# Sixty loads issued from ScalarE's program instead of SyncE's, with a new written order

## The chip, the cores and the metric

One core of a Trainium2 chip runs the whole kernel. The metric is the device time of one execution in microseconds (us), as the median of several runs. The engines are PE (TensorE, matrix products; PEld is its weight load), DVE (VectorE), ACT (ScalarE), POOL (GpSimd) and SP (SyncE), which here does nothing but issue DMA transfers. SPq is SP's program as the trace shows it.

## What is computed

Three layers in a row, in float32 precision (products are made from two-part float16 splits):

```python
# 1. delta rule attention; B, H, S, D = 4, 8, 768, 48
for t in range(S):
    y[:, :, t] = q_t @ state
    v_old = state^T @ k_t                       # k normalised
    state += beta_t * outer(k_t, v_t - v_old)
# 2. gated layer on x = y (S x 384): sigmoid(conv5(x)) * (x @ w_val) @ w_out
# 3. gated MLP: h = gelu(x @ w_in); u, v = halves of h; v = layernorm(v) * g
#    out = x + (u * (w_sg @ v + b)) @ w_out2     # w_sg mixes over the 768 positions
```

## The kernel before, in words

The attention is worked in chunks of 64 positions, 12 chunks to a batch element, 48 in all (`NSEQ`). All eight heads go together: four on each half of the 128 partitions. `norm` and `keys` prepare the keys of pairs of chunks (24 pairs, `ND`), `gram`, `base` and `merge` invert the small triangular systems of the chunks, `seq` carries the state from chunk to chunk, and `attend` gives the outputs, which go by a DMA (`xd<-ys`) to a buffer in memory. The MLP functions (`front`, `value`, `hidden`, `gates`, `mix`, `final`) read that buffer in tiles of 256 positions. Their products fill PE between the short products of the recurrence; in the last stretch of the run they are alone.

Three inputs are loaded all along the run: `kf` (keys, 12 loads, in `norm`), `qf` and `vf` (queries and values of a pair of chunks, 24 each, in `load`), 60 loads together. `qf` and `vf` have two buffers (`sp`, bufs=2), `kf` has one.

No scheduler decides the order. The class `Program` records every operation, and the table `ORDER` lists for each engine in which order it issues its operations. `in_order` replays this table with a model of costs, sorts the operations by their modelled starts, and puts filler products (`filler`, matrices `minus`, onto a scratch bank `ps_state`) where the model has PE idle. Each engine then runs its list in order on the chip, and an instruction that waits holds up all behind it on its engine. All recorded operations have one source line in the profile (L108 before, L109 after), so rows are told apart by tile names.

Names that recur below: `sq` are squares of the keys; `wst`, `wv` are staged weights; `rh`, `wh`, `ws`, `ps_q`, `ps_state` belong to the recurrence (`ws<-wh` is a DMA that spreads a result into a block frame); `m1p`, `tbd` are frames of the triangular inverses, filled by small DMAs from `gx`, `tah`; `ys` is the output tile of a pair and `xd` its buffer in memory; `kj` are key frames; `qh`, `mh` are split queries and scores.

Of the kernel before, what the change touches and what calls it, by code (L numbers as in the profile page):

```python
# [21 lines left out]
class Op:  # L22


    def __init__(self, index, engine, method, call, kw):
        self.index, self.engine, self.method, self.call, self.kw = index, engine, method, call, kw
        self.before, self.after, self.stage, self.due = set(), [], None, 0
        self.ready = self.end = 0.0
        self.blocks = engine == "tensor" and kw["lhsT"].shape[0] <= 64 == kw["lhsT"].shape[1]
        self.cost, self.time, self.port = cost(self)  # L30
# [9 lines left out]
class Program:  # L40
# [69 lines left out]
    def in_order(self):  # L110
# [14 lines left out]
        done, moved = [], 0.0  # L125
# [3 lines left out]
        def finish(op):  # L129
            for o in op.after:  # L130
                if o.engine != op.engine:
                    t = op.end + LATENCY[op.engine]
                elif op.engine == "tensor":
                    t = op.start
                else:
                    t = op.end + (LATENCY[op.engine] if op.engine == "sync" else 0.025)
                o.ready = max(o.ready, t)
                o.left -= 1

        while any(plan.values()):  # L140
            t, i = min((max(free[e], plan[e][0].ready), i) for i, e in enumerate(ENGINES) if plan[e] and not plan[e][0].left)
            e = ENGINES[i]
# [21 lines left out]
            if e in ("vector", "scalar"):  # L164
                if e in last and drains(last[e], op):
                    t = max(t, last[e].start + last[e].time)
                last[e] = op
            op.start, used, time = t, op.cost, op.time
            done.append(op)
            if e == "sync":  # L170
                used = max(used, moved - DMA_AHEAD - t)
# [41 lines left out]
class Pool:  # L213
# [5 lines left out]
    def tile(self, shape, dtype, name, tag=None, **kw):  # L219
# [326 lines left out]
def kernel(  # L546
# [32 lines left out]
    EP = C + E  # L579
# [816 lines left out]
```

## Time and profile before

| | |
|---|---|
| median of 3 runs | 647.62 us (646.28 to 649.8) |
| the profiled execution's own time | 646.62 us |
| its span in the profile | 644.7 us |
| PE busy | 575.0 us, 89% of the span |
| DVE busy | 503.1 us, 78% |
| ACT busy | 398.2 us, 62% |
| POOL busy | 179.6 us, 28% |
| DMA queue q1 (all issued by SP) | 87.72 MB, 63.0% of 16 engines' span |

Busy shares are means over stages that differ. PE does its first product at 20 us, and from there its share rises until it is nearly always busy. Issuing a DMA isn't counted as busy time, so SP has no line in the page; its issues are read from the timeline.

### The profile page before, as it was taken

What the parts mean: (1) busy time and instruction counts of PE and PEld (TensorE: products, weight loads), DVE (VectorE), ACT (ScalarE), POOL (GpSimd) and SP (SyncE); (2) the same over time, 40 slices, a digit from 0 to 9 for tenths busy, and PEclk for the clock granted to TensorE, in tenths of its full rate; (3) what the DMA queues carried; (4) which work ended last, traced back from release to release, by engine and by line L of the source; (5) the groups of instructions that cost most, each with busy time, mean ns of one, the idle gap of its engine ahead of it and who ended that gap; (6) DMA issues with size and microseconds to landing.
All of it is one profiled execution on the core that took longest, in us unless ns stands there. A gap on an engine that the chain in (4) does not pass through costs nothing. (4 is left out here: it accounts for less than half of the span.)

```text
span 644.7 us, 23559 instructions
## 1 busy us (share of the span) xinstructions
PE 575.0 (89%) x9821; PEld 473.8 (73%) x9821; DVE 503.1 (78%) x1341; ACT 398.2 (62%) x932; POOL 179.6 (28%) x204
## 2 busy tenths in 40 slices
PE   0678879779979989799999999889999999999997
PEld 0555446668767767688888689778978897877886
DVE  7898998979889998988999879899887854562222
ACT  7886697756876767775466785344948544524221
POOL 7404041126423625366001650001605010303000
PEclk9999998989999998999999999999999999999999
DMA  7664367877579776687678778788687763211121
GB/s 223 160 202 132 126 189 235 186 156 165 107 182 175 134 122 146 128 195 132 163 143 179 145 123 170 121 140 152 120 155 141 107 142 102 63 50 34 58 82 50
DMA packets 288826, 89.22 MB, mean 138 GB/s; under 512 B 250704, under 2 KB 276944, under 8 KB 288720
## 3 DMA queue, kind: packets, MB, share of 16 engines
q1 hardware_dynamic: 288720, 87.72, 63.0%
q8 instruction: 77, 1.26, 0.9%
q14 instruction: 29, 0.24, 0.1%
HBM read 51.81 MB, written 23.33 MB: 117 GB/s over the span
## 5 line engine op out<-in xcount | busy, mean ns | idle before, releaser
L108 PE MATMUL ps_mlp<-wg,vnh 128*128 128x256 f16 x864 | 112.4, 272 | 1.4 <-DVE ps_mlp L108 1.4
L108 PEld LDWEIGHTS <-vnh 128*128 128x128 f16 x864 | 80.5, 97 | 12.0 <-issue 2.1
L108 PEld LDWEIGHTS <-kj 112*128 112x128 f16 (+1 forms) x1632 | 69.2, 97 | 21.4 <-issue 12.7
L108 PEld LDWEIGHTS <-kc 64*64 64x64 f16 x1920 | 42.1, 113 | 47.5 <-DVE kc L108 20.8
L108 PE MATMUL ps_mlp<-gvh,wi 128*128 128x256 f16 x432 | 58.0, 272 | 1.2 <-ACT v L108 0.8
L108 PE MATMUL ps_mlp<-gth,w 128*128 128x256 f16 x432 | 58.8, 272 | 0.0
L108 DVE TENSOR_TENSOR tmp<-X 128x84 f32<-128x84 f32 (+12 forms) x156 | 56.1, 360 | 1.4
L108 DVE TENSOR_TENSOR X<-X,tmp 128x84 f32<-128x84 f32 (+12 forms) x156 | 54.5, 349 | 1.5
L108 PE MATMUL ps_mlp<-wi,gvh 128*128 128x512 f16 x216 | 54.7, 379 | 0.6 <-ACT gvh L108 0.4
L108 DVE SCALAR_TENSOR_TENSOR ps_mlp<-ps_mlp,gl,bs 128x256 f32<-128x256 f32 x48 | 23.4, 488 | 34.3 <-PE ps_mlp L108 33.9
L108 DVE SCALAR_TENSOR_TENSOR a<-x,cw,a 128x256 f32<-128x256 f32 x108 | 48.8, 486 | 1.6 <-ACT a L108 1.3
L108 PE MATMUL ps_mlp<-xh,wv 128*128 128x256 f16 x324 | 45.7, 272 | 2.2 <-ACT xh L108 2.1
L108 PE MATMUL ps_mlp<-gvh,wo 128*128 128x256 f16 x324 | 47.1, 272 | 0.1
L108 PEld LDWEIGHTS <-m1p 128*128 128x128 f16 x1152 | 39.5, 96 | 9.9 <-issue 5.7
L108 PE MATMUL pk<-i,kc 64*64 64x64 f16 x704 | 22.5, 200 | 27.2 <-DVE kc L108 20.0
L108 PEld LDWEIGHTS <-wi 128*128 128x128 f16 x432 | 40.3, 97 | 6.4 <-issue 1.3
L108 PEld LDWEIGHTS <-w 128*128 128x128 f16 x432 | 40.8, 98 | 5.0
L108 PE MATMUL ps_y<-qh,kj 112*128 112x64 f16 x576 | 32.8, 193 | 4.2 <-ACT ys L108 4.1
L108 POOL TENSOR_TENSOR X<-X,bm 128x1024 f32<-128x1024 f32 x5 | 11.8, 2353 | 87.4 <-DVE X L108 72.0
L108 PEld LDWEIGHTS <-ws 128*128 128x128 f16 (+1 forms) x828 | 32.2, 98 | 4.9 <-issue 3.2
L108 PEld LDWEIGHTS <-wo 128*128 128x128 f16 x342 | 31.8, 97 | 5.5 <-issue 0.9
L108 POOL TENSOR_TENSOR vnh<-v,vnh 128x512 f16<-128x512 f32 x24 | 27.9, 1170 | 25.6 <-ACT vnh L108 25.5
(165 smaller groups left out, 1451.5 us busy)
## 6 DMA issues: line engine op xcount, KB each, us to landing
keys_d<-kc SPq DMA_DIRECT2D x22, 512.0 KB, 4.1
kj<-keys_d SPq DMA_DIRECT2D x44, 256.0 KB, 5.0
wg<-wgd SPq DMA_DIRECT2D x12, 768.0 KB, 4.8
ws<-wh SPq DMA_DIRECT2D x66, 96.0 KB, 3.6
qf<-in_qt SPq DMA_DIRECT2D x24, 224.0 KB, 3.5
kf<-in_kn SPq DMA_DIRECT2D x12, 384.0 KB, 4.7
vf<-in_vn SPq DMA_DIRECT2D x24, 192.0 KB, 3.4
xd<-ys SPq DMA_DIRECT2D x48, 96.0 KB, 3.0
```

The costliest lines, as they stand in the source:

```text
L108: op.call()
```

## The change

The 60 loads of `kf`, `qf` and `vf` are issued by ScalarE (`nc.scalar.dma_start`) and no longer by SyncE. The model in `in_order` and `cost` learns that an operation can be a DMA on another engine than SP: it has the cost of a DMA, moves the same shared transfer clock, and isn't held back by transfers that are outstanding, as SP's are. `ORDER` has new tables for all engines. The frames (`tbd`, `m1p`, `ws`) are filled by GpSimd before and after. Per engine the counts are the same, but for the 60 loads (SP 60 fewer, ACT 60 more) and the fillers on PE: 268 before, 310 after, of which 140 and 128 are 128 rows high and the others 64.

```diff
+        self.dma = method == "dma_start"
...
-                    t = op.end + LATENCY[op.engine]
+                    t = op.end + LATENCY["sync" if op.dma else op.engine]
...
-            if e in ("vector", "scalar"):
+            if e in ("vector", "scalar") and not op.dma:
...
-            if e == "sync":
-                used = max(used, moved - DMA_AHEAD - t)
+            if op.dma:
+                used = max(used, moved - DMA_AHEAD - t) if e == "sync" else used
...
 ORDER = dict(
     tensor=(
-        "17:12 0 29:2 1 31 2 32 3:14 113 65:2 129:13 67 142 68 114 143 115 69 144 116:3 70 119 71 120 72 121 73 122 "
+        "0 17:14 1 31 2 32 3:14 65:5 129:6 113 135:2 114 137:7 115 144 116:4 70:2 120:2 72:2 122:4 74:3 126:2 49:3 "
...
-    out, engine = op.kw["out"], op.engine
+    out, engine = op.kw["out"], "sync" if op.dma else op.engine
...
-                nc.sync.dma_start(out=kf[:, 2 * i:2 * i + 4], in_=kn_f[:, k * n + 2 * i:k * n + 2 * i + 4])
+                nc.scalar.dma_start(out=kf[:, 2 * i:2 * i + 4], in_=kn_f[:, k * n + 2 * i:k * n + 2 * i + 4])
...
-        nc.sync.dma_start(out=qf[0:EP], in_=qt_f[:, n:n + 2])
+        nc.scalar.dma_start(out=qf[0:EP], in_=qt_f[:, n:n + 2])
...
-        nc.sync.dma_start(out=vf, in_=vn_f[:, n:n + 2])
+        nc.scalar.dma_start(out=vf, in_=vn_f[:, n:n + 2])
```

First place: the start of ACT's program. Before:

```order
1 L108 ACT_TABLE_LOAD
2 L108 ACTIVATE wh_109<-zero 128x512
3 L108 ACTIVATE sq<-kf 128x384
4 L108 ACTIVATE kj_91<-zero 128x1024
5 L108 ACTIVATE sq<-kf 128x384 x2
```

After:

```order
1 L109 DMA kf<-in_kn 128x768
2 L109 DMA vf<-in_vn 128x384
3 L109 DMA qf<-in_qt 112x512
4 L109 DMA kf<-in_kn 128x768
5 L109 DMA vf<-in_vn 128x384
6 L109 DMA qf<-in_qt 112x512
7 L109 ACT_TABLE_LOAD
8 L109 ACTIVATE wh_109<-zero 128x512
9 L109 ACTIVATE sq<-kf 128x384 x2
10 L109 ACTIVATE kj_91<-zero 128x1024
```

Six loads now stand ahead of the table load, and the second `sq` has moved ahead of the clearing of `kj`.

Second place: SP's program where the outputs of a pair in the third batch element are stored (`xd_81<-ys`, two DMAs to a pair). Before:

```order
326 L108 DMA vf<-in_vn 128x384
327 L108 DMA tbd_95<-tah 32x16x32
328 L108 DMA ws_97<-wh_109 64x16x48
329 L108 DMA xd_81<-ys 48x4x128
330 L108 DMA ws_97<-wh_109 64x16x48
331 L108 DMA qf<-in_qt 112x512
332 L108 DMA bs<-in_b_sg 128x256
333 L108 DMA tbd_94<-tah 32x16x32
334 L108 DMA xd_81<-ys 48x4x128
```

After:

```order
270 L109 DMA ws_97<-wh_109 64x16x48
271 L109 DMA tbd_95<-tah 32x16x32
272 L109 DMA xd_81<-ys 48x4x128 x2
273 L109 DMA ws_97<-wh_109 64x16x48
274 L109 DMA wg<-wgd 128x3072
275 L109 DMA bs<-in_b_sg 128x256
```

The two loads are gone from the row, and the two stores follow each other directly, where four issues stood between them.

Third place: ACT's program in the middle of the recurrence, around the two results `wh<-ps_q` and `wh<-ps_state` of a chunk. Before:

```order
642 L108 ACTIVATE mh<-ps_y 128x256
643 L108 ACTIVATE rh<-ps_q 128x192
644 L108 ACTIVATE bs<-bs 128x256
645 L108 ACTIVATE tbd_95<-ps_b 32x8x32
646 L108 ACTIVATE wh_109<-ps_q 128x4x48
647 L108 ACTIVATE wh_109<-ps_state 112x4x48
```

After:

```order
691 L109 ACTIVATE mh<-ps_y 128x256
692 L109 ACTIVATE rh<-ps_q 128x192
693 L109 DMA vf<-in_vn 128x384
694 L109 DMA qf<-in_qt 112x512
695 L109 ACTIVATE wh_109<-ps_q 128x4x48
696 L109 ACTIVATE tbd_95<-ps_b 32x8x32
697 L109 ACTIVATE bs<-bs 128x256
698 L109 ACTIVATE wh_109<-ps_state 112x4x48
```

Two loads stand between `rh` and the `wh` that follows from it, where two other activations stood before.

## Rows read from the trace of the kernel before

**Rows 1.** Page, part 1: busy time of each engine, share, instructions.

```profile
PE 575.0 (89%) x9821; PEld 473.8 (73%) x9821; DVE 503.1 (78%) x1341; ACT 398.2 (62%) x932; POOL 179.6 (28%) x204
```

**Rows 2.** Windows: stretch, PE, PEld, DVE, ACT, POOL busy (instructions), clock, DMA share, GB/s.

```profile
20.00:280.00 260.00, 223.15 (x4563) 172.11 (x4564) 230.28 (x635) 190.03 (x461) 91.11 (x95) 0.98 0.70 160
280.00:520.00 240.00, 232.19 (x4065) 200.12 (x4063) 208.41 (x553) 151.13 (x354) 62.68 (x61) 1.00 0.78 148
520.00:645.00 125.00, 119.67 (x1203) 101.59 (x1199) 48.78 (x109) 41.89 (x85) 12.98 (x14) 0.99 0.23 66
```

**Rows 3.** Waits of PE from 20 to 280 us: total us, times, longest.

```profile
PE pk L108 <- ACT kc L108: 4.3, 8, 0.8
...
PE ps_y L108 <- ACT ys L108: 2.7, 5, 0.9
PE ps_mlp L108 <- DMA wsf<-in_w_sgT: 2.2, 2, 1.6
...
PE ps_b L108 <- DMA m1p<-gx: 1.1, 1, 1.1
```

**Rows 4.** Waits of PE from 280 us to the end.

```profile
PE ps_b L108 <- DMA m1p<-gx: 2.7, 2, 1.4
PE ps_y L108 <- DMA ws<-wh: 1.9, 3, 1.4
PE ps_y L108 <- ACT ys L108: 1.4, 2, 0.7
...
PE ps_q L108 <- DMA kj<-keys_d: 0.5, 1, 0.5
```

**Rows 5.** Waits of DVE from 20 to 280 us.

```profile
DVE wh L108 <- ACT wh L108: 4.5, 7, 1.5
DVE wst L108 <- ACT wst L108: 3.8, 4, 1.5
```

**Rows 6.** SP's issues of the three loads: min/median/max ns, first and last start.

```profile
L108 SPq DMA_DIRECT2D kf<-in_kn x12: 333/423/3324, 0.8 to 263.5; - x12
...
L108 SPq DMA_DIRECT2D qf<-in_qt x24: 328/446/1677, 5.0 to 523.3; - x24
...
L108 SPq DMA_DIRECT2D vf<-in_vn x24: 358/560/2043, 3.6 to 498.9; - x24
```

**Rows 7.** SP's timeline at the second place: start us, us, issue.

```profile
464.14 0.59 SPq L108 DMA_DIRECT2D vf<-in_vn  x1
...
468.88 0.60 SPq L108 DMA_DIRECT2D qf<-in_qt  x1
...
470.85 0.62 SPq L108 DMA_DIRECT2D xd<-ys  x1
```

**Rows 8.** ACT's and PE's timeline there, [idle before <-releaser].

```profile
474.81 0.38 ACT L108 ACTIVATE ys<-ps_y 112x256 f32<-112x256 f32 x1 [2.54 <-DMA xd<-ys]
...
475.24 0.51 PE L108 MATMUL ps_y<-qh,kj 112*128 112x64 f16 x12 [0.74 <-ACT ys L108]
```

**Rows 9.** Waits of SP's own queue, whole span.

```profile
SPq L108 <- ACT qh L108: 9.8, 6, 3.9
...
SPq L108 <- DVE qh L108: 6.3, 1, 6.3
```

**Rows 10.** Timelines of the start: ACT, SP, DVE, PE.

```profile
0.80 1.28 ACT L108 ACT_TABLE_LOAD   x1 [0.80 <-PEq L1383]
...
3.98 0.52 ACT L108 ACTIVATE sq<-kf 128x384 f32<-128x384 f32 x1 [0.77 <-DMA kf<-in_kn]
...
1.71 0.43 SPq L108 DMA_DIRECT2D beta_sb<-in_beta  x1
2.19 0.43 SPq L108 DMA_DIRECT2D gl<-in_g_ln  x1
...
16.61 0.56 DVE L108 SCALAR_TENSOR_TENSOR wst<-wst 128x384 int32<-128x384 int32 x1 [1.73 <-ACT wst L108]
...
20.04 0.53 PE L108 MATMUL pk<-i,kc 64*64 64x64 f16 x12 [20.04 <-DVE kc L108]
```

**Rows 11.** Fillers on PE: line, operation, count, busy us, mean ns, idle before.

```profile
L108 PE MATMUL ps_state<-minus 128*128 128x256 f16 (+1 forms) x268 | 30.9, 278 | 0.5 <-DVE wh L108 0.5
```

More of the change, by code (lines that the diff above doesn't have):

```diff
@@ L135, in finish @@
                 else:
-                    t = op.end + (LATENCY[op.engine] if op.engine == "sync" else 0.025)
+                    t = op.end + (LATENCY["sync"] if op.dma else 0.025)
                 o.ready = max(o.ready, t)
```

391 rows, old and new, of tables (gpsimd, scalar, sync, tensor) are left out of this document.

## The prediction

> **What bounds the kernel now.** I read the page's busy shares first: PE is busy for 575.0 of 644.7 us, and no other engine above 78% [rows 1]. The table by windows then splits the span into three stages [rows 2]. From 20 to 280 us PE is busy for 223.15 of 260 us and DVE for 230.28; ACT has 190.03, that is 73%, and neither PE nor DVE is alone the limit: both wait for links of the recurrence. From 280 to 520 us PE has 232.19 of 240 us, and after 520 us 119.67 of 125 us. So from 280 us on the time is PE's own work, of which this change takes nothing away; what can move is the first 20 us, the 36.9 us in which PE stands between 20 and 280 us, and the 7.8 us until 520 us.
>
> The waits of PE say what these are made of. Early, the largest that ACT causes are 4.3 us for `kc` and 2.7 us for `ys`, and those for transfers are 2.2 us (`wsf`) and 1.1 us (`m1p`) [rows 3]. Late, transfers are most of it: `m1p` 2.7, `ws` 1.9, `kj` 0.5, and 1.4 us for `ys` [rows 4]. That `ys` is really a transfer: at one of its places ACT stands for 2.54 us until the store `xd<-ys` has landed, and PE then stands 0.74 us for ACT [rows 8]. DVE's early waits for ACT are led by 4.5 us (`wh`) and 3.8 us (`wst`) [rows 5].
>
> **The change part by part.** The planner's edited lines run before the program exists and cost the chip nothing. Bytes and shapes of the transfers stay.
>
> *SP loses 60 issues.* At the medians of their rows, 12 `kf` at 0.423, 24 `qf` at 0.446 and 24 `vf` at 0.560 us are 5.1 + 10.7 + 13.4 = 29.2 us off SP's program [rows 6]. SP isn't the limit by itself; it is worth what PE waits behind SP's transfers: 2.2 + 1.1 early, 2.7 + 1.9 + 0.5 + 1.4 late, 9.8 us together [rows 3, 4]. That is the upper bound of the gain; the lower is nothing, since a shorter queue doesn't make a transfer later. In between, the place that I followed: in the 6.7 us ahead of the store at 470.85 us SP issued a `vf` and a `qf`, 0.59 and 0.60 us each [rows 7]; without them the store goes out 1.2 us earlier, more than PE's 0.74 us there [rows 8], and in the new order the two stores have nothing between them. But only every eighth issue is a load, so not each wait has one ahead of it. I take -4.0 us, two fifths of the bound.
>
> [...]
>
> *ACT gains 60 issues.* No row shows an issue on ACT. The nearest are SP's: 0.33 us at the least, 0.42 to 0.56 at the median, 3.32 at the most [rows 6]. I take 0.43 us, as the first lone issues of the run took [rows 10]. Six stand at the start (below); the other 54 are spread evenly over the chunks, up to 523 us [rows 6], so about 54 x 260/503 = 28 fall between 20 and 280 us (12 us more on ACT) and 26 behind it. Early, PE's 4.3 + 2.7 and DVE's 4.5 + 3.8 us of waits stand against 190 us of ACT's work, 0.08 us for each us of work [rows 2, 3, 5]: 1.0 us. Some stand inside the recurrence, as the two between `rh` and `wh` at the third place, so I take +1.5 us. The bounds: if the loads only fill ACT's idle quarter, 0; if each lies on the path wherever ACT is busy, 12 x 0.73 = +9. Behind 280 us PE's own queue of MLP products hides them: PE is busy for 97% there [rows 2]; without that cover it would be 26 x 0.43 = 11 us.
>
> A wait moves with each load: its buffer must be free. On SP such waits are in the queue's list, 9.8 us for ACT's own `qh` and 6.3 us for DVE's [rows 9]. The first kind is free on ACT, whose program has passed it. The second kind would now hold what is behind the load: at the third place `wh`, for which PE and DVE wait. I cost it at nothing, since loads have some 20 activations between them and can stand late; if it bites, it is the second rival.
>
> *The start.* `kf` goes out at the same moment as before, but six issues of 0.43 us, 0.48 apart [rows 10], put the table load 2.9 us later, its end at 5.0, and with the 0.5 us of `wh` the first `sq` at 5.5 us instead of 3.98 [rows 10]: +1.5 us. The second `sq` then follows at once, and ACT's 0.77 us wait for `kf` is gone. The start ends with a chain: DVE stands 1.73 us until ACT has made `wst` (16.61 us), after which the keys are scaled and PE begins at 20.04 us [rows 10]. ACT's lateness reaches that chain unless it is regained by ACT's pauses. I take +1.0 us, bounds 0 and +1.5.
>
> *The new order and the fillers.* There are 42 more fillers; one keeps PE for 30.9 / 268 = 0.115 us [rows 11]. They stand in gaps, cost nothing there, and at most 4.8 us where a gap isn't one. What the other moved rows do I can't sum up; the products are the same. With 24 pairs of chunks and a quarter of a us won or lost at each, 6 us either way. I take 0.
>
> The sum: -4.0 + 1.5 + 1.0 + 0 = -1.5 us on the profiled execution's 646.62 us, 645.1. That execution was 1.0 us below the median of the runs, 647.62; on the median it is 646.1 us, which I predict.
>
> **The rivals.** *The relief counts in full and the order regains more* (faster). All 9.8 us of waits behind SP's transfers go, and ACT's issues vanish in its pauses, which the early stage has (27% of the time). The start takes 1.0 back and a shorter chain gives a little: about 638 us. For it: SP issues without pause at the places of the late waits. Against it: the early stage, with most of PE's idle time, hardly waits for transfers.
>
> *ACT is held up* (slower). One mechanism: an issue on ACT takes as long as SP's in a crowded stretch or longer, and activations of the recurrence wait behind it. Place: 20 to 280 us. Price: 28 issues of 0.65 us are 18 us, of which half comes through to PE over `rh`, `wh` and `kc`, +9, with the start +1.5 and a relief of only 2: about 656 us. It decides from a mean issue on ACT of about 0.6 us, or a few of 2 to 3 us as SP's longest [rows 6]. For it: DMA engines are 70 to 78% busy there [rows 2], and DVE's waits for ACT lead its list. Against it: ACT has idle time, and the loads aren't urgent. [...]
>
> *SP isn't relieved* (the change doesn't do what it says). SP's long issues come from the crowd of transfers, which stays; then the remaining issues stretch, the gain is 0, and 1.5 + 1.0 are left: about 650 us. For it: 0.33 us alone and 0.6 in a crowd [rows 6, 7].
>
> **How the numbers follow.** A measurement of this kernel can tell about 0.5%, 3.2 us, from no change: faster is below 644.4, slower above 650.9. The forecast as summed has 0.44, with its own range 641 to 651.5: 0.12 of it faster, 0.29 the same, 0.03 slower. The fast rival has 0.25, the held-up ACT 0.20, the unrelieved SP 0.11 (0.06 the same, 0.05 slower). Faster 0.37, same 0.35, slower 0.28. The range goes from 635, a little beyond the fast rival, to 657, which takes in the slow one.
>
> **What would show it.** Right: issues on ACT of about 0.4 us; PE's late waits for `m1p`, `ws` and `ys` down from 6.0 us to about 3; PE's first product at about 21 us; PE busy for 223 us or a little more between 20 and 280 us. Wrong: issues on ACT above 0.6 us, with ACT's waits replaced by longer gaps ahead of `wh` and `rh` and PE's waits for ACT doubled (second rival); SP's issues longer than before, and late waits unchanged (third); or PE's idle time between 20 and 280 us changed by over 5 us with neither, which would be the order's doing and is what my sum knows least of.

## The result and the profile after

The changed kernel takes 649.43 us (median of 20 runs, 644.93 to 657.06), the kernel before 645.67 us in its 20 runs beside it. The ratio is 1.0051 with a 95% interval of 1.003 to 1.0071: 3.3 us slower (here and below, a ratio is turned into us on 645.67). Ratios leave out the runs over 1.5% above the fastest of their kernel, so they can differ from the ratio of the medians. The forecast was 646.1 us, 1.5 us faster than the 647.62 us that it was worked out on. The profiled execution took 649.55 us, with a span of 647.7, 3.0 above that of the kernel before.

Part 1 of the page answers to [rows 1]:

```profile
PE 579.0 (89%) x9863; PEld 476.2 (74%) x9863; DVE 498.5 (77%) x1341; ACT 398.1 (61%) x932; POOL 179.5 (28%) x204
```

The windows, columns as in [rows 2]:

```profile
20.00:280.00 260.00, 219.67 (x4512) 168.76 (x4513) 223.76 (x620) 188.13 (x458) 89.23 (x97) 0.96 0.69 159
280.00:520.00 240.00, 235.94 (x4098) 203.04 (x4098) 211.76 (x569) 153.93 (x360) 66.21 (x63) 1.00 0.82 147
520.00:648.00 128.00, 122.97 (x1254) 104.32 (x1252) 51.85 (x114) 44.11 (x90) 13.16 (x14) 1.00 0.24 69
```

Between 280 and 520 us PE's idle time fell from 7.81 to 4.06 us, 3.75 less: near the 4.0 that the forecast gave to the relief of SP. But the first stage lost 3.5 us of PE time, and the end has 3.3 us more work left in it. The waits of PE from 280 us on answer to [rows 4]; `m1p` and `kj` are gone, and `m1p`, `ws` and `ys` fell from 6.0 to 2.3 us:

```profile
PE ps_y L109 <- ACT ys L109: 1.4, 2, 0.8
PE ps_y L109 <- DMA ws<-wh: 0.9, 1, 0.9
```

The start answers to [rows 10]. ACT's timeline (start us, us):

```profile
0.80 0.40 ACTq L109 DMA_DIRECT2D kf<-in_kn  x1
1.23 0.45 ACTq L109 DMA_DIRECT2D vf<-in_vn  x1
1.70 0.45 ACTq L109 DMA_DIRECT2D qf<-in_qt  x1
2.19 0.45 ACTq L109 DMA_DIRECT2D kf<-in_kn  x1
4.62 0.33 ACTq L109 DMA_DIRECT2D vf<-in_vn  x1
6.67 0.34 ACTq L109 DMA_DIRECT2D qf<-in_qt  x1
7.04 1.28 ACT L109 ACT_TABLE_LOAD   x1 [7.04 <-DMA vf<-in_vn]
8.34 0.63 ACT L109 ACTIVATE wh<-zero 128x512 f32<-128x512 f32 x1
8.87 0.51 ACT L109 ACTIVATE sq<-kf 128x384 f32<-128x384 f32 x1
```

and PE's first product:

```profile
22.82 1.06 PE L109 MATMUL pk<-i,kc 64*64 64x64 f16 x32 [16.34 <-DVE kc L109]
```

Four loads go out 0.43 to 0.49 us apart, as forecast. Then ACT stands until 4.62 and again until 6.67 us. The table load comes 6.2 us later than before, the first `sq` 4.9 and PE's first product 2.8. What ACT stands for is a semaphore. In the trace the 485 transfers that SP and ACT issue share eight semaphores for their landings, used in turn: the first eight transfers have one each, and the ninth to the thirteenth wait for those of the first to the fifth. The first `kf` landed at 4.60 and the first `vf` at 6.65 us, each 0.02 us before ACT's next load began. The built order of ACT shows the waits:

```
4 L109 DMA kf<-in_kn 128x768
5 L109 DMA vf<-in_vn 128x384 [waits DMAHW0_49]
6 L109 DMA qf<-in_qt 112x512 [waits DMAHW2_49]
7 L109 ACT_TABLE_LOAD
```

SP's `wsf` and `bs` are held in the same way, for 2.1 us to 4.78 (`beta_sb` landed at 4.77) and for 1.8 us to 6.94 (`wst`, at 6.93). Before, such holds at the start came to 0.3 us, ahead of `bs`: SP, at 0.39 to 0.46 us for each of its first twelve issues, began the ninth to the twelfth 0.14 to 0.60 us after the landings that free their semaphores, and ACT issued none.

In the run an issue on ACT took 0.34 to 0.35 us at the median of each kind (min/median/max ns), where [rows 6] had 0.42 to 0.56 on SP:

```profile
L109 ACTq DMA_DIRECT2D qf<-in_qt x24: 318/335/452, 1.7 to 507.8; - x24
...
L109 ACTq DMA_DIRECT2D vf<-in_vn x24: 334/350/457, 1.2 to 503.0; - x24
...
L109 ACTq DMA_DIRECT2D kf<-in_kn x12: 334/353/613, 0.8 to 271.2; - x12
```

SP's other 425 issues took 317.6 us together, before 315.1 (median 0.63 and 0.62 us): hardly any of the 40.7 us that the loads had taken on SP passed on to them.

### The profile page after: what moved, and what is told of

Its sections match the earlier page's. It is cut to its first block, busy times and chain, and to the rows that moved or that the text cites. A ratio compares the mean times of both kernels' runs of the same rounds, so it can differ in the third digit from the quotient of the medians.

```text
span 647.7 us, 23605 instructions
## 1 busy us (share of the span) xinstructions
PE 579.0 (89%) x9863; PEld 476.2 (74%) x9863; DVE 498.5 (77%) x1341; ACT 398.1 (61%) x932; POOL 179.5 (28%) x204
## 4 chain that ended last, share of the span: by engine, by line
PE 62%; DVE 14%; ACT 9%; DMA 7%; issue 4%; SPq 2%; POOL 1%; ACTq 1%; DVEq 0%; POOLq 0%
PE ps_mlp L109 42%; PE ps_y L109 6%; PE pk L109 4%; PE ps_q L109 4%; DVE X L109 3%; PE ps_state L109 3%; PE ps_b L109 3%; DMA xd<-ys 2%; DVE tmp L109 2%; SPq L109 2%; ACT kc L109 1%; DVE wst L109 1%; DMA vf<-in_vn 1%; DMA tbd<-tah 1%; DMA ws<-wh 1%
## 5 line engine op out<-in xcount | busy, mean ns | idle before, releaser
L109 PE MATMUL ps_mlp<-wg,vnh 128*128 128x256 f16 x864 | 111.0, 272 | 0.6 <-DVE ps_mlp L109 0.6
L109 PE MATMUL ps_mlp<-gvh,wi 128*128 128x256 f16 x432 | 55.3, 272 | 1.2 <-ACT v L109 0.8
L109 PE MATMUL ps_state<-minus 64*64 64x256 f16 (+1 forms) x310 | 34.4, 294 | 7.0 <-POOL minus L109 6.1
L109 POOL TENSOR_TENSOR rd<-va,root 128x2 f32<-128x2 f32 x12 | 8.8, 734 | 96.9 <-DVE va L109 96.9
```

Of the source, the lines that this page charges most:

```text
L109: op.call()
```

## The experiments

Each is timed beside runs of the kernel before on its own chip; given are the median, the ratio to the kernel before and its 95% interval. By the intervals a difference between two of these kernels is known to 2 to 4 us. A single profile places a cost only roughly: b_late below has the program of before, unchanged until 281 us, and yet was 4.2 us ahead of it at 271 us. Where loads move in the lists, the planner sets the fillers anew: 290 in e_move and b_move for 268 before, 320 in e_lift and 334 in e_quiet for 310 in e_start.

**The start.** Two edits of the changed kernel. e_start has the first six loads on SP, in SP's old order (`nc.scalar if n > 2 else nc.sync`, keys `if k`), the other 54 on ACT. e_four only moves ACT's fifth and sixth load behind the first two `sq`, the clearing of `kj` and the first `rh` in ACT's list.

> The changed kernel with its first six loads on SP, in the old order of SP's first twelve issues; the other 54 stay on ACT. Theory S: the table load at 0.80 us and PE at about 20 us, 2.8 us faster than the changed kernel, and with the late waits for transfers that the move removed as fast as before or up to 3 us faster. Theory O and theory A: the table load as early, but the time only 0 to 1 us better than the changed kernel.

Measured: 646.87 us, 1.0015 [0.9986, 1.0045]. ACT's timeline begins as before, and PE's first product comes at 19.69 us:

```profile
0.80 1.28 ACT L109 ACT_TABLE_LOAD   x1 [0.80 <-PEq L1374]
...
3.96 0.94 ACT L109 ACTIVATE sq<-kf 128x384 f32<-128x384 f32 x2 [0.75 <-DMA kf<-in_kn]
...
19.69 1.06 PE L109 MATMUL pk<-i,kc 64*64 64x64 f16 x32 [13.22 <-DVE kc L109]
```

> The changed kernel with one edit in ACT's order: of its first six loads the fifth and sixth (vf and qf of the second pair) stand behind the first two sq, the clearing of kj and the first rh. Theory S (the start): these two wait until a completion semaphore that an earlier transfer uses is free again, and hold the table load until 7.04 us. Without them ahead of it the table load starts at about 2.7 us and PE at about 20.5 us instead of 22.82; 2.3 to 2.8 us faster than the changed kernel, about 1 us above the kernel before. Theory O (the new order itself costs the time): start earlier, but the time stays 2 to 4 us above before. Theory A (issues on ACT cost the time in the recurrence): the same as theory O.

Measured: 647.33 us, 1.0029 [0.9997, 1.006]; table load at 2.68, PE's first product at 21.2 us. By the middles of the intervals the two held loads cost about 1.4 us and the whole start 2.3 (from 1.0051 to 1.0015), most of the loss; the intervals overlap. PE's first product agrees: 22.82 us falls by 1.6 without the held loads, and by 1.5 more in e_start. That second part has two changes in it, the other four loads off ACT and SP's old order of the first transfers, and e_order below shows that the order counts.

**The two halves apart.** e_order is the new order with all 60 loads on SP at their planned times; e_move is the old order with all 60 on ACT where SP had issued them; b_move is e_move with the first six left on SP.

> The new order with all 60 loads on SP again, put in where the planner's replay of the new order has them; ACT's list without them, so that the table load stands first. Theory S: PE starts at about 20 us, the time within 1 us of before. Theory O: 3 to 4 us slower than before, as the changed kernel. Theory A: as before.

Measured: 655.7 us, 1.0168 [1.0117, 1.022]. Against the expectation PE began late, though ACT's table load starts at 0.80 us: the second `kf` goes out as SP's sixth transfer, not its second, and ACT's third and fourth `sq` stand for it.

```profile
10.34 0.94 ACT L109 ACTIVATE sq<-kf 128x384 f32<-128x384 f32 x2 [1.82 <-DMA kf<-in_kn]
...
21.83 1.07 PE L109 MATMUL pk<-i,kc 64*64 64x64 f16 x32 [15.36 <-DVE kc L109]
```

So with no load on ACT the new order of the first transfers already starts PE 1.8 us late.

> The loads on ACT in the order of the kernel before: SP's list without the 60 loads, ACT's list with each put in where the planner's replay of the old order has it; all other lists as before. At the start three loads stand ahead of the table load. Theory S: the table load is late by about 1.4 us only, the time 0 to 1.5 us above before. Theory O: as before, or 2 to 4 us faster than before, since SP is relieved and the order is the old one. Theory A: 3 to 5 us slower than before, as the changed kernel.

Measured: 653.79 us, 1.0123 [1.0075, 1.0171].

> The kernel before, its own order, with the first six loads left on SP as before and the other 54 on ACT at the places where SP issued them: the move alone without the start. e_move, with the first six on ACT too, was 1.0123 [1.0075, 1.0171]. The parts measured so far: ACT's time for 54 places +0.2 to +1.4 (b_act, 1.0021), the 24 late loads 1.0009 (b_late). Theory 'the parts add, and the rest of e_move is its start': 1.000 to 1.004 (0 to +2.5 us). Rival 'the 30 loads between cost by themselves in the old order, by what they meet on the other queue and by frames that are not free': 1.006 to 1.012 (+4 to +8).

Measured: 651.72 us, 1.0103 [1.0058, 1.0148]: the rival with a cost by itself. So the order with SP as issuer costs 10.8 us (about 1.8 of them its start) and the loads alone 6.7 (with the fillers set anew), but both together, without the start, 1.0. Neither part gains anything; each loses less where the other is. The windows of e_order say that in the new order with SP as issuer the late relief isn't there (PE busy 232.38, before 232.19), and that PE is busy for 6 us less in the early stage, the late start included:

```profile
20.00:280.00 260.00, 217.15 (x4461) 167.39 (x4461) 220.75 (x609) 184.20 (x448) 90.28 (x97) 0.97 0.66 154
280.00:520.00 240.00, 232.38 (x4032) 200.06 (x4029) 211.33 (x570) 154.65 (x362) 66.16 (x63) 1.00 0.79 149
```

and those of e_start that with ACT as issuer it is (235.35):

```profile
20.00:280.00 260.00, 222.62 (x4552) 171.68 (x4548) 223.68 (x625) 187.97 (x457) 90.52 (x99) 0.96 0.69 158
280.00:520.00 240.00, 235.35 (x4090) 202.60 (x4090) 209.58 (x560) 152.18 (x355) 64.82 (x62) 1.00 0.80 149
```

A difference of 1.5 us in such a window says nothing: b_act below, with every load on SP, has 233.74 there.

**Early loads, late loads.** In the new order n_late gives the 24 loads behind 282 us back to SP, n_early the 30 between the start and there (both with e_start's start); in the old order b_late gives only the 24 late ones to ACT.

> The version with the first six loads on SP (e_start, 1.0015 of before), with the 24 query and value loads of sequences 24 and on (from 282 us) given back to SP at their planned times; ACT keeps the 30 loads between. In e_start the pairs' lag behind the kernel before falls from +4.9 at 271 us to -0.4 at 479 us. Theory 'the late relief is the new order's own' (with all loads on SP in the new order, e_order, the lag still fell by 4.6; with ACT as the issuer in the old order, b_late, it did not fall): the fall stays at 4 or more, the time within 1.5 us of e_start, ratio 0.999 to 1.004. Theory 'the late relief is SP's, as the forecast had it' (-4.0): the fall is 1 or less, the time 3 to 4 us above e_start, ratio 1.006 to 1.008.

Measured: 649.62 us, 1.0079 [1.004, 1.0117], so 4.1 us above e_start. The time is that of SP's relief. The place wasn't as that theory had it: the lag of the pairs (how much later ACT writes the same pair's `ys` than in the kernel before) still fell by 4.2 us from 271 to 479 us, and PE's idle time of 280 to 520 us is 5.59 against e_start's 4.65 us. The expectation was split, and the mark of the place was a poor one: e_order and n_early show the same fall (4.6 and 5.8 us), so it belongs to where the new order puts its pairs, not to the issuer.

> The counterpart of n_late: e_start with the 30 loads between the first six and sequence 24 (keys of the later sets, queries and values up to 262 us) given back to SP at their planned times; ACT keeps the 24 late ones. All loads on SP in the new order (e_order) cost 8.8 more than e_start, and by the pairs' lag most of it came before 271 us (+12.3 against +4.9). Theory 'in the new order the issuer matters before 280 us': +5 to +8 on e_start, ratio 1.009 to 1.014. Rival 'it matters after 280 us' (the forecast's place): within 2 us of e_start, ratio 0.999 to 1.004.

Measured: 650.82 us, 1.0083 [1.0051, 1.0115], 4.4 us above e_start, between the two theories. With n_late it makes 8.5 of the 9.8 us between e_order and e_start; both start PE at 19.8 us, so e_order's late start is not in them. In the new order the issuer is worth about as much early as late, as far as differences known to 3 us can tell.

> The kernel before with its own order, and only the 24 query and value loads of the second half (sequences 24 and on, issued from 281 us on) given to ACT, at the place in ACT's list where SP issued them. The first 281 us are as before. Theory 'the relief belongs to the issuer': -3 to -4 (ratio 0.994 to 0.9955), PE idle 280-520 us from 7.8 to about 4 us. Rival 'ACT pays for it where its list was not drawn for it' (the move alone in the old order, e_move, cost +7.9 and had PE idle 280-520 us at 7.1): 0 to +4 (ratio 1.000 to 1.006), PE idle 280-520 us at 7 us or more and DVE's waits for ACT's wh and m1p up.

Measured: 644.34 us, 1.0009 [0.998, 1.0039], PE's idle time of 280 to 520 us at 8.19 us: no relief shows in the old order (1.3 us at the most by the interval). PE's waits for `ws` rose in its trace, from 1.9 [rows 4] to 4.8 us, as those for `m1p` fell from 2.7 to 1.1:

```profile
PE ps_y L109 <- DMA ws<-wh: 4.8, 3, 2.1
PE ps_b L109 <- DMA m1p<-gx: 1.1, 1, 1.1
```

**What SP's and ACT's issues cost.** b_act is the kernel before, with no load moved, and at each of the 54 places of b_move two ACTIVATEs of 8 columns that nobody reads. b_split is the kernel before with 54 loads cut in two halves by partitions, e_split is e_start cut likewise:

```
+                if op.dma and op.engine == "scalar":
+                    h = op.kw["out"].shape[0] // 2
+                    for s in (slice(0, h), slice(h, 2 * h)):
+                        op.call(out=op.kw["out"][s], in_=op.kw["in_"][s])
```

> The kernel before, with its own order and SP as issuer of every load, and two ACTIVATEs of 8 columns (about 0.2 us each by the trace's ACTIVATEs of 15 columns, 199 ns) that nobody reads, added on ACT's list at each of the 54 places where the move alone (e_move) had a load: 54 x 0.4 = 21.6 us of ACT time, as 54 issues with what stands around them take, and no load moved. It prices what ACT pays by itself. Theory 'ACT's in-order time is on the path' (e_move cost +8 in all, of which start about 1.5): +5 to +10, ratio 1.008 to 1.016. Forecast (B, +1.5 for 60): 0 to +2, ratio 1.000 to 1.003.

Measured: 646.98 us, 1.0021 [0.9984, 1.0058]: 1.4 us by the middle of the interval, for 16.0 us of ACT's time, 199 ns each:

```profile
L114 ACT ACTIVATE extra<-eye 128x8 f16<-128x8 f32 x108 | 16.0, 199 | 0.1
```

The forecast's term for ACT's time (+1.5) fits, and by itself it isn't what b_move pays.

> The kernel before, its order and SP as the issuer of all 60 loads, with the 54 loads after the first six each cut into two halves by partitions: 54 issues more on SP, the same bytes. Theory 'SP's issue time is on the path after 280 us' (the forecast's term A, -4.0 for 60 issues taken off): +3.6 or more, ratio 1.0055 to 1.014, PE idle 280-520 us from 7.8 to 11 us or more, with its waits for ws and m1p up. Rival 'SP has room, and the relief seen in the changed kernel is the order's': within 1 us, ratio 0.999 to 1.002, PE idle 280-520 us at about 8 us.

Measured: 654.48 us, 1.0164 [1.0128, 1.02]; PE's idle time of 280 to 520 us rose from 7.81 to 11.55 us. SP's issues are on the path: 10.6 us for 54 more, above the forecast's 4.0 for 60 and just above its bound of 9.8. SP issued for 42.7 us longer (398.5 us in all, before 355.8), 33.8 of them on the loads: a half took 0.57 to 0.59 us at the median. Behind the start no issue on SP began within 0.2 us of the landing that frees its semaphore, so it isn't the turn of the semaphores that costs here. Whether some of it comes from the halves' transfers and not from their issues isn't separated.

> The version with the first six loads on SP (e_start, 646.87, 1.0015 of before), with each of the 54 loads that ACT issues cut into two halves by partitions: 54 issues more on ACT, the same bytes. Theory 'an issue on ACT costs what it takes' (0.335 us each by the trace of the changed kernel, on ACT's in-order path): up to 54 x 0.335 = 18 us of ACT time, of which the forecast's own share for 60 issues (+1.5, at most +9) would give +1.4 to +8 on e_start, so 648.3 to 655 and a ratio of 1.004 to 1.014. Theory 'an issue on ACT lies beside the ACTIVATE before it': within 1 us of e_start, ratio 1.000 to 1.003, and PE's waits for ACT unchanged.

Measured: 670.64 us, 1.0421 [1.0379, 1.0463], outside both theories, and it doesn't price an issue. The halves of `vf` and `kf` took longer to issue than the whole loads, and ACT stood for landings, once for 3.88 us (to 463 us, for one of `vf`):

```profile
L112 ACTq DMA_DIRECT2D qf<-in_qt x44: 321/343/1356, 17.3 to 528.1; - x44
L112 ACTq DMA_DIRECT2D vf<-in_vn x44: 472/494/1337, 106.3 to 523.3; - x44
...
L112 ACTq DMA_DIRECT2D kf<-in_kn x20: 472/618/1577, 33.2 to 278.5; - x20
```

Of the 108 issues, 15 began within 0.2 us of an update of the semaphore that they use, after pauses of ACT of 8.9 us together; in e_start it is 4 of 54. So with these 54 transfers more the turn of the semaphores held ACT in the run too.

**What the run loses.** e_fill is e_start with the planner's constant for fillers at 0.45 in place of 0.55 (205 fillers, not 310). e_lift is e_start with the 12 loads before which ACT stood moved later in its list. b_quiet and e_quiet are b_move and e_start with 26 and 30 loads moved later to places behind which SP issued few small transfers.

> e_start with the planner's constant for filler products at 0.45 in place of 0.55: 204 fillers instead of 309 (all of the missing ones before 280 us), everything else in the same order. Theory 'the fillers take PE time from the work' (0.11 us each by the trace, 105 fewer): -4 to -11 on e_start, ratio 0.985 to 0.996. Theory 'they stand in idle time and hold the clock up': +1 to +6, with the granted clock of 20 to 280 us below e_start's 0.95 to 0.97. Theory 'neither': within 1 us of e_start (ratio 1.000 to 1.003).

Measured: 649.78 us, 1.0069 [1.0029, 1.0108], 3.5 us slower than e_start. The granted clock, as a share of full speed, was 0.982 on the mean of the compared runs against 0.989, and over the runs of either kernel 0.01 of it went with 3.3 to 3.4 us: 2.4 of the 3.5 us. By that the fillers hold the clock up, and no cost of theirs shows; the other 1.1 us is within the interval.

> e_start (1.0015 of before) with 12 of ACT's 54 loads moved 2 to 8 ACT instructions later in ACT's list: those before which ACT stood in the trace of e_start for 0.27 to 1.78 us, 8.6 us in all (2.7 of it at 211 to 237 us), because the frame that the load fills was not yet free (GpSimd's qh ends five of these). Nothing else is moved. Theory 'a load in ACT's list that meets a full frame holds ACT's program, and that is on the path': standing before loads near 0, -2 to -5 on e_start, ratio 0.994 to 0.999. Rival 'ACT stood beside other waits': standing gone, the time within 1 us of e_start, ratio 1.000 to 1.003. Against both: a load that lands later makes its reader late, over 1.004.

Measured: 647.59 us, 1.0004 [0.9971, 1.0037]; ACT's standing before loads went from 8.6 us to nothing above 0.25, the time by 0.7 us. ACT stood beside other waits: the rival.

> b_move (old order, first six loads on SP, the other 54 on ACT; 1.0103 of before, +6.6 us), with 26 of the 54 loads moved later in ACT's list (within 9 us and before their readers need them) to places behind which SP issued few of its small transfers in b_move's trace: SP's issues of ws, m1p, tbd and xd in the 2.5 us behind a load fall from 96 (m1p and xd counted twice) to 32 by that trace. In the trace of b_move such a transfer landed 2.2 us (m1p) and 3.15 us (ws) after its issue's end, and 3.3 and 4.2 with a load from ACT under way in front of it. Theory 'loads on a queue of their own run ahead of SP's small transfers, and these land about 1 us later': half of the 6.6 us or more comes back, ratio 1.000 to 1.006. Rival 'the cost is ACT's time or the frames': the ratio stays at 1.008 to 1.013.

Measured: 652.01 us, 1.0094 [1.0055, 1.0133]. In the trace the transfers with a load in front (one issued less than 2.5 us before and still under way) fell for `m1p` from 10 to 7, `ws` from 21 to 12, `tbd` from 23 to 13, and the time stayed: the rival.

> The same in the new order: e_start (1.0015 of before) with 30 of its 54 ACT loads moved later to places behind which few small transfers stood in its trace (103 to 33 by the same count). Theory 'loads run ahead of SP's small transfers': -2 to -4 on e_start, ratio 0.995 to 0.999, m1p's, ws's and xd's landings with a load in front fewer than e_start's 6, 16 and 18. Rival 'the new order has already placed the loads where it costs nothing': within 1 us of e_start, ratio 1.000 to 1.003. Against both: loads that land too late for their readers, over 1.004.

Measured: 652.13 us, 1.0098 [1.0066, 1.013], 5.4 us slower than e_start. This falls under "against both", though not by late loads alone: ACT's waits for `bs` rose from 2.7 to 5.9 us and PE's for `m1p` from 0.9 to 2.0. The places of the loads in the new order are worth more than the rule by which I moved them.

## Why the prediction was wrong

*The start* is the term that failed first. "ACT's lateness reaches that chain unless it is regained by ACT's pauses. I take +1.0 us, bounds 0 and +1.5" counted six issues of 0.43 us and nothing between them. The last two stand 2.0 and 1.7 us for a landing, PE began at 22.82 instead of about 21 us, and the start cost 2.3 us by the runs (e_start), 2.8 by the profile. The waits stood in the built order, which I had read for rows and not for what each waits for. The held loads are a bit over half of it (e_four). The term also left out the new order of the first transfers: that "`kf` goes out at the same moment as before" held for the first `kf` only, and with all loads on SP this order alone began PE 1.8 us late (e_order). What the four loads ahead of the table load cost apart from that is open.

*The new order, "I take 0"*, with *SP's 60 issues, -4.0*: the two aren't terms that can be added. The time taken off SP was not the fault: the loads' issues came to 40.7 us of SP's program, more than the 29.2 that their medians give, and hardly any of it passed on to other issues. But with SP as issuer the order costs +10.8 (e_order); ACT as issuer then takes 9.8 off (to e_start), of which about 2.1 us are PE's earlier start. That this is the upper bound of the relief to the digit is chance. From the other side, ACT as issuer costs +6.7 in the old order (b_move), where the forecast's -4.0 + 1.5 had a gain, and the order then takes 5.7 off. Either way 1.0 us is left where the sum had -2.5. With the start's 2.3 that makes the 3.3 us measured. That SP's issues are on the path was right (b_split); that taking them off is worth 4 us in any order was not (b_late, b_move). The late stage's 3.75 us, so near the forecast's 4.0, are luck in so far as they came in the new order alone.

*ACT's 60 issues, +1.5*, fits: 0.34 to 0.35 us an issue, and -1.0 to 3.7 us by b_act's interval. *Fillers*: no cost of theirs shows (e_fill), as taken, at 34.4 us of them in place of 30.9 [rows 11]:

```profile
L109 PE MATMUL ps_state<-minus 64*64 64x256 f16 (+1 forms) x310 | 34.4, 294 | 7.0 <-POOL minus L109 6.1 <-ACT wh L109 0.9
```

Of the signs, issues of 0.4 us and late waits of about 3 us (2.3) came; PE's first product at 21 us and PE busy for 223 us early (219.67) didn't. PE's early waits for `kc` went from 4.3 [rows 3] to 7.0 us. That is the order's doing and not the loads' on ACT, as the traces of e_order (no load on ACT) and then of b_move (54 of them, the old order) show:

```profile
PE pk L109 <- ACT kc L109: 7.0, 10, 1.4
...
PE pk L109 <- ACT kc L109: 3.6, 7, 0.8
```

Of the rivals, "ACT is held up" named the right engine for the start alone, with the wrong mechanism. ACT was held by the landing of an earlier transfer (at 4.60 and 6.65 us), not by long issues: the longest in the run was 0.61 us, and 46 of the 60 ran while SP was issuing too, at a median of 0.34 us like the other 14. These durations show no wait of ACT's issues for SP's. The third rival's sign, longer issues on SP, didn't come either.

What stays open: why the 30 loads between the start and 281 us cost about 6 us on ACT in the old order. It is hardly ACT's time (b_act) nor the late loads (b_late), and moving the loads out of the small transfers' way brought nothing (b_quiet). The 22 more fillers, at 0.12 us each, are 2.6 us at the most. The granted clock isn't it: over b_quiet's runs it was 0.988 on the mean, as beside them in the kernel before, and the loss stayed. By the profiles the loss of b_move lies between 190 and 304 us (1.9 to 7.2 us behind), as far as single profiles can place it. Open too is by what the new order loses with SP as issuer. No version that ran beats the kernel before; the nearest, e_lift and b_late, are equal to it within their intervals.

## What to carry to other kernels

A load moved to another engine's program takes its waits along, also those that the build adds: here SP's and ACT's transfers use eight semaphores in turn, and of six loads at the head of ACT's program the last two stopped ACT for 2.0 and 1.7 us until earlier transfers had landed. Read the built program's waits for the moved instructions, not only their order. An order that was searched for one assignment of work to engines can't be priced as a separate term: price it with the assignment, or run both crosses before you add. An edit that gives work back to its old engine often changes the order as well; look at where each version's first products begin before you subtract.

## What the runs showed that I had not expected

- A load's issue took 0.34 to 0.35 us on ACT, less than SP's 0.42 to 0.56; half of a load by partitions took longer than the whole (`vf` 494 ns in e_split against 352 in e_start, `kf` 618 in e_split against 353 in the changed kernel).
- 54 more issues on SP, of halves of loads, cost 10.6 us, while 108 more small ACTIVATEs on ACT, busy for 62% of the time, cost 1.4.
- With a load in front, some small transfers landed later after the end of their issue: in the kernel before 3.55 against 2.90 us (`ws`, means of 21 and 51) and 2.93 against 2.23 (`tbd`, 29 and 67); for `m1p` no difference shows (2.30 against 2.22, 10 and 38). No run shows that the load is the cause.
